# Moving nearly all 128x128 transposes from TensorE to the DMA engines, with two residual buffers and an earlier load of Wo

## The chip, the cores and the metric

One core of one Trainium2 chip runs the whole program in one launch. The metric is the device time in microseconds (us), and lower is better.

Engine names as the profile has them: PE is TensorE's matmul side, PEld its weight load, DVE is VectorE, ACT is ScalarE, POOL is GpSimd, SP is SyncE. SP issues the DMAs here, and "SPq" marks the time an issue holds SP's sequencer.

## The reference

The program is four layers on a sequence of 2048 tokens with 640 features, in the order A, B, A, B. Each is a residual layer on a layer norm.

```python
x = x + A(layernorm(x)); x = x + B(layernorm(x)); x = x + A(layernorm(x)); x = x + B(layernorm(x))

def A(x):                      # 32 heads of 20 features, 4 segments of 512 tokens
    for s in range(4):
        p = softmax(qs @ ks.T * scale + mask);  a_dot = p @ vs
        pq = phi(qs); a_mem = (pq @ M) / (pq @ z + 1e-6)
        o = g * a_mem + (1 - g) * a_dot         # g = sigmoid(beta), per head
        pk = phi(ks); M = M + pk.T @ vs; z = z + sum(pk)
    return o @ wo              # phi(t) = t + 1 if t > 0 else exp(t)

def B(x):                      # 32 heads of 128, 64 steps of 32 tokens, 8 memory tokens
    for s in range(64):
        h = concat(mem, xs); q, k, v = h @ Wq, h @ Wk, h @ Wv
        o = (softmax(q @ k.T * scale + mask) @ v) @ Wo
        mem = o[:8]; outs.append(o[8:])         # the next step needs this one's output
```

## The kernel before

Everything is bf16 except the accumulations. A layer A is 32 units, each one segment for four heads, and a unit is six slots. The kernel fixes the order of the instructions on PE, ACT, DVE and POOL. So an instruction that waits also holds up everything behind it on its engine, although nothing else in the program needs it (the timeline after the change shows such a case: ACT idle for 4.09 us before the exp of K, with the exp of the last scores behind it). SP is a fifth, in-order queue, which issues nearly all DMAs (in that unit the transpose of K is issued 3.28 us late, behind four others).

The projection of the next unit, and K's feature map with its transposes:

```python
def proj(u, k):                                   # k = 0: Q, k = 1: K
    PP = pg.tile([128, 512], F32, name="a_PP", tag="pg")
    for c in range(NCH):                          # NCH = 5
        nc.tensor.matmul(PP[:], lhsT=wts[u][k][:, c, :], rhs=xnTs[n % 2][:, c, :], ...)
    nc.vector.tensor_copy(U.qk[:, k, :], PP[:])   # "evacuation" of K when k = 1
    ...
def phi_k(u):                                     # not in the last segment
    KN = pg.tile([128, 4, 128], BF16, name="a_KN", tag="pg")
    for tt in range(4):
        nc.tensor.transpose(KN[:, tt, :], U.qk[:, 1, 128 * tt:128 * tt + 128], C.identb[:])
    EK = ...; nc.scalar.activation(out=EK[:], in_=KNv, func=ACT.Exp)
    t1 = ...; nc.vector.tensor_scalar(out=t1[:], in0=KNv, ...)          # max(k + 1, 1)
    nc.vector.tensor_tensor(out=phik[u % 2][...], in0=EK[:], in1=t1[:], op=ALU.min)
```

The schedule of a unit, with `extras` standing for norms, V projections and output projections that are spread over the slots:

```python
for slot in range(6):
    score(u, slot)                                # a_S on PE, exp into a_PT on ACT
    if slot == 0: proj(u + 1, 0)
    if slot == 1: pvmm(u - 1, 1); norm(u - 1)
    if slot == 2: proj(u + 1, 1); phi_q(u + 1)
    if slot == 4: pvmm(u, 0); phi_k(u + 1)
    if slot == 5: nummm(u); memory(u)             # a_UP on PE, then a_um on DVE
    extras(u, slot)
```

The PSUM pool `pg` is shared by `a_PP`, `a_KN`, `a_UP` and the transposes. Norms (`a_tps`), attention outputs (`a_otps`) and B's norms (`b_lntps`) are transposed on PE in the same way, then copied out of PSUM by ACT. B loads its residual into the one tile `XO` in mid-step, and holds the first 11 of 32 heads of Wo early (`NW1 = 11`).

Of the kernel before, what the change touches and what calls it, by code (L numbers as in the profile page):

```python
# [26 lines left out]
NW1 = 11  # L27
# [171 lines left out]
def layer_A(nc, nc_raw, tc, C, W, A_wv, A_wo, x_src, x_dst, xb_dst, src_is_bf16, general, outer, mem0, prep=None, prefetch=()):  # L199
# [5 lines left out]
    with ExitStack() as ctx:  # L205
# [19 lines left out]
        Onat = so.tile([128, 4, D], BF16, name="a_Onat")  # L225
# [41 lines left out]
        def ln_tr(nc, xn, n, tt):  # L267
            tps = pg.tile([128, NCH, 128], BF16, name="a_tps", tag="pg")
            for c in range(NCH):
                nc.tensor.transpose(tps[:, c, :], xn[:, 128 * c:128 * c + 128], C.identb[:])  # L270
            nc.scalar.copy(xnTs[n % 2][:, :, 128 * tt:128 * tt + 128], tps[:])
# [24 lines left out]
        eps = so.tile([128, 2, 4, 4], F32, name="a_eps")  # L296
# [3 lines left out]
        for tt in range(5):  # L300
            if tt < 4:
                stats[tt] = ln_stats(nc, xts[tt])
            if tt > 0:
                ln_tr(nc, ln_apply(nc.vector, xts[tt - 1], *stats[tt - 1]), 0, tt - 1)
# [9 lines left out]
        gg = W.gates(nc, so)  # L314
        build_masks(nc, C)

        def run(gctx):
# [14 lines left out]
            wl = wk1 if general else wk  # L332
# [15 lines left out]
            def phi_q(u):  # L348
                if u // NG == 0:
                    return  # L350
                U = us[u]
                t1 = wl.tile([128, 512], BF16, name="a_t1q", tag="t1")
                nc.vector.tensor_scalar(out=t1[:], in0=U.qk[:, 0, :], scalar1=1.0, scalar2=1.0, op0=ALU.add, op1=ALU.max)
                nc.vector.tensor_tensor(out=U.phiq[:], in0=U.phiq[:], in1=t1[:], op=ALU.min)

            def phi_k(u):
                if u // NG == NS - 1:
                    return
                U = us[u]
                KN = pg.tile([128, 4, 128], BF16, name="a_KN", tag="pg")  # L360
                for tt in range(4):
                    nc.tensor.transpose(KN[:, tt, :], U.qk[:, 1, 128 * tt:128 * tt + 128], C.identb[:])
                KNv = KN[:].rearrange("p t (j s) -> p t j s", s=32)[:, :, :, 0:20]
                EK = wl.tile([128, 4, 4, 20], BF16, name="a_EK")
                nc.scalar.activation(out=EK[:], in_=KNv, func=ACT.Exp)
                t1 = wl.tile([128, 4, 4, 20], BF16, name="a_t1k", tag="t1")
                nc.vector.tensor_scalar(out=t1[:], in0=KNv, scalar1=1.0, scalar2=1.0, op0=ALU.add, op1=ALU.max)
                nc.vector.tensor_tensor(out=phik[u % 2][:, :, :, 0:20], in0=EK[:], in1=t1[:], op=ALU.min)

            def row_max(u):  # L370
# [19 lines left out]
                ms = wl.tile([12, 512], BF16, name="a_ms", tag="t1")  # L390
# [58 lines left out]
            def norm(u):  # L449
                n, G = divmod(u, NG)  # L450
                K = 2 if n else 1
                pv = us[u].pv
                r = so2.tile([128, 2, 4, 4], F32, name="a_r")
                nc.vector.tensor_tensor(out=r[:, 0:K], in0=pv[:, 0:K, :, :, 20], in1=eps[:, 0:K], op=ALU.add)
                i = so2.tile([128, 2, 4, 4], F32, name="a_i")
                nc.vector.reciprocal(out=i[:, 0:K], in_=r[:, 0:K])
                if not general:
                    watch(nc, C, r[:, 0].rearrange("p t j -> p (t j)"), i[:, 0].rearrange("p t j -> p (t j)"))
                q = so2.tile([128, 2, 4, 4], F32, name="a_q")
                nc.vector.tensor_tensor(out=q[:, 0:K], in0=i[:, 0:K], in1=gg[:, 0:K, 4 * G:4 * G + 4].unsqueeze(2).to_broadcast([128, K, 4, 4]), op=ALU.mult)  # L460
                Ov = Onat[:, :, 80 * G:80 * G + 80].rearrange("p t (j d) -> p t j d", d=20)
                if n == 0:
                    nc.vector.tensor_tensor(out=Ov, in0=pv[:, 0, :, :, 0:20], in1=q[:, 0].unsqueeze(3).to_broadcast([128, 4, 4, 20]), op=ALU.mult)
                else:
                    ts = so.tile([128, 2, 16, 20], F32, name="a_ts")
                    nc.vector.tensor_tensor(out=ts[:].rearrange("p k t d -> p (k t) d"), in0=pv[:].rearrange("p k t j s -> p (k t j) s")[:, :, 0:20],
                                            in1=q[:].rearrange("p k t j -> p (k t j)").unsqueeze(2).to_broadcast([128, 32, 20]), op=ALU.mult)
                    tv = ts[:].rearrange("p k (t j) d -> p k t j d", j=4)
                    nc.gpsimd.tensor_tensor(out=Ov, in0=tv[:, 0], in1=tv[:, 1], op=ALU.add)
                us.pop(u)  # L470

            def memory(u):
# [9 lines left out]
                else:  # L482
                    um = wk1.tile([128, 4, 21], F32, name="a_um", tag="a_EK" if general else "a_um")
# [4 lines left out]
            def chunk(c):  # L488
                tps = pg.tile([128, 4, 128], BF16, name="a_otps", tag="pg")
                for tt in range(4):  # L490
                    nc.tensor.transpose(tps[:, tt, :], Onat[:, tt, 128 * c:128 * c + 128], C.identb[:])
                nc.scalar.copy(oT[:, c, :], tps[:].rearrange("p t q -> p (t q)"))
# [28 lines left out]
            def bridge_ops(G, slot):  # L521
# [15 lines left out]
                if (G, slot) == (5, 4):  # L537
                    xn, m0 = ln["b"]
                    tps = pg.tile([128, NCH, 128], BF16, name="a_btps", tag="pg")
                    for c in range(NCH):  # L540
                        nc.tensor.transpose(tps[:, c, :], xn[:, 128 * c:128 * c + 128], C.identb[:])
                    nc.scalar.copy(br.xnT[:], tps[:])
# [16 lines left out]
            def extras(u, slot):  # L559

                n, G = divmod(u, NG)
                if n >= 1 or u >= NU:
                    if (G, slot) == (0, 0):
                        chunk(3)
                        if u < NU:
                            res_load(n - 1, 0); res_load(n - 1, 1)
                    elif (G, slot) == (1, 0):
                        chunk(4)
# [10 lines left out]
                seq = {(4, 0): 0, (5, 0): 1, (6, 0): 2}  # L579
                if (G, slot) in seq:  # L580
                    chunk(seq[G, slot])
# [19 lines left out]
            proj(0, 0); proj(0, 1); phi_q(0); phi_k(0)  # L601
            if general:
                row_max(0)
            for u in range(NU + 1):
# [7 lines left out]
                for slot in range(6):  # L612
# [7 lines left out]
                    if slot == 2 and more:  # L620
                        proj(u + 1, 1)
                        phi_q(u + 1)
# [10 lines left out]
            br.tail = [lambda: chunk(4)] + [lambda i=i: outp(NS - 1, i) for i in range(8)]  # L633
# [27 lines left out]
def layer_B(nc, nc_raw, tc, C, W, br, outer, wo_src, x_src, xb_src, x_dst, general, nsteps=64, out_bf16=False):  # L661
# [4 lines left out]
    with ExitStack() as ctx:  # L666
# [43 lines left out]
        def ln_tr(g):  # L710
            xn = ln_n.pop(g)
            tps = pot.tile([128, NCH, 128], BF16, name="b_lntps", tag="ot")
            for c in range(NCH):
                nc.tensor.transpose(tps[:, c, :], xn[:, 128 * c:128 * c + 128], C.identb[:])
            xg = wk2.tile([128, NCH, 128], BF16, name="b_xnTg")
            nc.scalar.copy(xg[:], tps[:])
# [157 lines left out]
        XO = st.tile([64, 320], F32, name="b_XO")  # L874
        nc.vector.memset(XO[:], 0.0)
# [38 lines left out]
        for a, b in ((NW1, 22), (22, 32)):  # L914
# [18 lines left out]
        for s in range(nsteps):  # L933
            last = (s == nsteps - 1)
            T, i4 = divmod(s, 4)
            if i4 == 0 and T >= 1:
                load_deferred(T - 1)
# [182 lines left out]
            for jj2 in range(2):  # L1120
                nc.sync.dma_start(XO[32 * jj2:32 * jj2 + 24, :], x_src[32 * s:32 * s + 24, 320 * jj2:320 * jj2 + 320])
# [51 lines left out]
            def store(s=s, ops=ops):  # L1173
# [123 lines left out]
```

## Time and profile before

| | before |
|---|---|
| median (lowest to highest) of its 4 runs | 2296.64 us (2293.05 to 2297.84) |
| profiled run (2302.5 us, another run than these four): span, mean granted clock | 2300.8 us, 0.981 |
| first A, first B, second A, second B | 263.2, 830.9, 266.1, 846.1 us |
| the two joins from A to B | 22.0, 21.1 us |

The stage lengths are worked out from the timeline. An A runs from its first to its last score matmul (`a_S`), a join from there to B's first matmul (`b_Qa`), and what is missing from the span is the start of the program and the passage from B to A (28.5 and 22.9 us).

The page of the kernel before: busy time by engine, PE's granted clock in 40 slices of the span, in tenths (9 is full or nearly so), and the chain of waits that ended last, by engine.

```profile
PE 2195.3 (95%) x54988; PEld 1234.9 (54%) x54988; DVE 1623.6 (71%) x3996; ACT 961.6 (42%) x2207; POOL 1028.5 (45%) x2475
...
PEclk9999989999999999999999999999999999999999
...
PE 81%; DVE 8%; ACT 5%; issue 3%; DMA 2%; SPq 1%; POOL 0%; DVEq 0%; ACTq 0%; POOLq 0%
```

At 95% PE looks like the only limit. By windows it is not. The next fence has the first A, the first join with most of the first B, and the second A of the kernel before. The columns are the window, its length, and busy us (with instructions) of PE, PEld, DVE, ACT and POOL, then PE's granted clock, the DMA share and GB/s.

```profile
28.50:291.70 263.20, 241.28 (x2747) 128.40 (x2747) 193.37 (x490) 199.51 (x276) 118.61 (x301) 0.97 0.53 150
293.00:1140.00 847.00, 836.75 (x24538) 475.70 (x24539) 601.32 (x1459) 275.05 (x818) 389.06 (x926) 0.99 0.10 28
1167.60:1433.60 266.00, 243.67 (x2746) 129.07 (x2746) 195.28 (x484) 197.38 (x270) 116.32 (x280) 0.96 0.34 107
```

In B, PE is nearly full (836.75 of 847 us here). In A it is idle for 22 us of each layer, and no other engine is full. There the unit is a cycle of waits through PE, DVE and ACT. The timeline of one unit of the second A shows it (start, duration, engine, line, operation, written and read tiles, count, and in brackets the idle time before it and what ended it).

```profile
1251.19 0.68 DVE L85 CAST a_qk<-a_PP 128x512 bf16<-128x512 f32 x1
...
1252.25 0.38 PE L85 MATMUL a_KN<-c_identb,a_qk 128*128 128x128 bf16 x4
...
1252.67 0.44 ACT L85 ACTIVATE a_EK<-a_KN 128x320 bf16<-128x320 bf16 x1
...
1253.00 0.81 ACT L85 ACTIVATE a_PT<-a_S 128x768 bf16<-128x768 f32 x1
...
1253.85 0.42 DVE L85 TENSOR_TENSOR a_PT<-a_PT,a_tri 128x512 bf16<-128x512 bf16 x1
...
1254.19 0.24 DVE L85 TENSOR_TENSOR a_um<-a_UP,a_bd 128x84 f32<-128x84 f32 x1
...
1254.61 1.25 PE L85 MATMUL a_PP<-a_xnT,a_wt 128*128 128x512 bf16 x5
```

K is evacuated at 1251.87 (1251.19 plus 0.68). PE transposes it, and ACT's exp of K starts at 1252.67, 0.80 us after the evacuation. Behind it on ACT is the exp of the last scores (1253.00 to 1253.81), and behind that on DVE the mask (1253.85) and `a_um` (1254.19), which frees a PSUM buffer for the next projection `a_PP`. Five projection matmuls take 1.25 us here.

### The profile page before, as it was taken

How to read it: one execution, taken by the hardware profiler on the slowest of the kernel's cores; microseconds unless marked ns; L12 is line 12 of the kernel's file. 1: busy time of each engine (PE TensorE's matmuls, PEld its weight loads, DVE VectorE, ACT ScalarE, POOL GpSimd, SP SyncE). 2: the span in 40 equal slices, each digit the busy share in tenths (PEclk: the TensorE clock that was granted, in tenths of full speed). 3: DMA queues.
4: the chain of work that ended last, by engine and by line, in shares of the span. 5: the costliest groups of instructions: out<-in, count | busy, mean ns of one | idle time of the engine just before them, and what ended most of it. 6: DMA issues, size and time to landing. Idle time of an engine off the chain costs nothing.

```text
span 2300.8 us, 123029 instructions
## 1 busy us (share of the span) xinstructions
PE 2195.3 (95%) x54988; PEld 1234.9 (54%) x54988; DVE 1623.6 (71%) x3996; ACT 961.6 (42%) x2207; POOL 1028.5 (45%) x2475
## 2 busy tenths in 40 slices
PE   6998989999999999999889989899999999999997
PEld 3444545555555555555445445455555555555554
DVE  5777757777777777776667777577777777777775
ACT  5777823333333333333267667233323333333332
POOL 3344534444444444444323445344444444444442
PEclk9999989999999999999999999999999999999999
DMA  6455540000000000000123333400000000000000
GB/s 168 138 147 166 164 143 21 20 21 19 20 19 20 20 22 20 22 15 18 49 89 119 105 108 119 147 19 15 18 15 17 16 19 16 17 18 16 14 13 15
DMA packets 90652, 123.40 MB, mean 54 GB/s; under 512 B 16496, under 2 KB 80000, under 8 KB 88192
## 3 DMA queue, kind: packets, MB, share of 16 engines
q1 hardware_dynamic: 87648, 111.84, 16.9%
q8 instruction: 431, 7.06, 1.3%
q10 hardware_dynamic: 2464, 3.61, 0.6%
q14 instruction: 109, 0.89, 0.1%
HBM read 89.17 MB, written 26.21 MB: 50 GB/s over the span
## 4 chain that ended last, share of the span: by engine, by line
PE 81%; DVE 8%; ACT 5%; issue 3%; DMA 2%; SPq 1%; POOL 0%; DVEq 0%; ACTq 0%; POOLq 0%
PE b_V L85 13%; PE b_OPS L85 12%; PE b_tail L85 10%; PE b_Qa L85 6%; PE b_Kb L85 6%; PE b_Ka L85 6%; PE b_Qb L85 6%; PE b_SP L85 5%; PE a_PP L85 4%; ACT a_PT L85 4%; PE b_OTL L85 3%; PE b_OPSd L85 3%; PE a_S L85 2%; PE a_pv L85 2%; DVE a_qk L85 1%
## 5 line engine op out<-in xcount | busy, mean ns | idle before, releaser
L85 PEld LDWEIGHTS <-b_hT 128*32 128x32 bf16 x15120 | 372.3, 96 | 311.3 <-DVE b_hT L85 69.2
L85 ACT ACTIVATE b_PT<-b_SP 128x224 bf16<-128x224 f32 x256 | 92.3, 361 | 765.5 <-PE b_SP L85 744.7
L85 PE MATMUL b_V<-b_wv,b_hT 128*32 128x512 bf16 x5040 | 356.3, 381 | 0.0
L85 ACT ACTIVATE a_PT<-a_S 128x768 bf16<-128x768 f32 (+1 forms) x384 | 326.4, 893 | 62.8 <-PE a_S L85 56.1
L85 PE MATMUL b_OPS<-b_wo,b_OTsb 128*32 128x320 bf16 x8192 | 329.3, 302 | 6.5 <-DVE b_OTsb L85 5.1
L85 PEld LDWEIGHTS <-b_OTsb 128*32 128x32 bf16 x8192 | 200.4, 97 | 94.9 <-DVE b_OTsb L85 47.5
L85 POOL CAST b_QT<-b_TQ 128x384 bf16<-128x384 f32 x254 | 140.3, 552 | 231.5 <-DVE b_TQ L85 231.5
L85 ACT CAST b_OTsb<-b_OTL 128x320 bf16<-128x320 f32 x384 | 150.9, 427 | 198.9 <-PE b_OTL L85 183.1
L85 POOL TENSOR_TENSOR b_PT<-b_PT,b_R 128x64 bf16<-128x64 bf16 x256 | 107.3, 419 | 221.8 <-ACT b_R L85 197.4
L85 POOL CAST b_KT<-b_TQ 128x384 bf16<-128x384 f32 x254 | 142.6, 561 | 136.8 <-DVE b_TQ L85 132.1
L85 PE MATMUL b_Qa<-b_wq,b_hT 128*32 128x512 bf16 x2520 | 183.2, 384 | 5.0 <-DVE b_hT L85 5.0
L85 POOL TENSOR_SCALAR_AFFINE_SELECT a_PT<-a_PT 128x256 bf16<-128x256 bf16 x256 | 108.2, 424 | 174.2 <-ACT a_PT L85 162.1
L85 PE MATMUL b_Kb<-b_wk,b_hT 128*32 128x512 bf16 x2520 | 182.9, 380 | 0.1
L85 PE MATMUL b_Ka<-b_wk,b_hT 128*32 128x512 bf16 x2520 | 182.2, 382 | 0.0
L85 DVE STREAM_TRANSPOSE b_TM<-b_OPS 128x128 f32<-128x128 f32 x252 | 88.2, 350 | 123.6 <-PE b_OPS L85 119.7
L85 PE MATMUL b_Qb<-b_wq,b_hT 128*32 128x512 bf16 x2520 | 158.3, 379 | 0.0
L85 PE MATMUL a_PP<-a_xnT,a_wt 128*128 128x512 bf16 x560 | 146.5, 394 | 5.1 <-DVE a_um L85 1.3
L85 PE MATMUL a_S<-a_qk 32*128 32x512 bf16 (+3 forms) x1024 | 137.2, 308 | 8.1 <-ACT a_PT L85 6.9
L85 DVE CAST b_Vsb<-b_V 128x512 bf16<-128x512 f32 x128 | 88.6, 692 | 76.8 <-PE b_SP L85 48.0
L85 DVE CAST b_OTsb<-b_OTL 128x320 bf16<-128x320 f32 x128 | 62.9, 492 | 98.2 <-PE b_OTL L85 98.2
L85 DVE TENSOR_TENSOR b_PT<-b_PT,b_R 128x160 bf16<-128x160 bf16 x256 | 104.0, 406 | 37.7 <-PE b_V L85 18.6
L85 POOL TENSOR_TENSOR b_Rtot<-b_Rtot,b_R 128x160 bf16<-128x160 bf16 x256 | 126.6, 494 | 0.0
(165 smaller groups left out, 4276.0 us busy)
## 6 DMA issues: line engine op xcount, KB each, us to landing
a_wt<-a_wpad SPq DMA_DIRECT2D x112, 160.0 KB
b_XO<-xres SPq DMA_DIRECT2D x256, 30.0 KB
a_wvo<-in_A_wo_dram SPq DMA_DIRECT2D x8, 800.0 KB
b_wq<-in_B_Wq_dram SPq DMA_DIRECT2D x20, 256.0 KB
b_wk<-in_B_Wk_dram SPq DMA_DIRECT2D x20, 256.0 KB
xres<-a_xo SPq DMA_DIRECT2D x16, 320.0 KB
xres_bf<-a_xb SPq DMA_DIRECT2D x32, 160.0 KB
b_wv<-in_B_Wv_dram SPq DMA_DIRECT2D x20, 256.0 KB
```

The source lines that it names most:

```text
L85: r = f(*a, **k)
```

## The change

The intent is to free PE of its transposes and ACT of the copies behind them. Every norm in A (but those of the prologue), every K, all attention outputs, and the norms in B go through a transposing DMA on SP, 136 in all, from SBUF to SBUF. B's residual has two buffers, loaded at the start of a step, and 16 heads of Wo are loaded early instead of 11. Tiles move between pools to make room. The core of the diff, with cuts marked:

```diff
-NW1 = 11
+NW1 = 16
 ...
-        def ln_tr(nc, xn, n, tt):
+        def ln_tr(nc, xn, n, tt, dma=True):
+            dst = xnTs[n % 2][:, :, 128 * tt:128 * tt + 128]
+            if dma:
+                nc_raw.sync.dma_start(dst, xn[:], transpose=True)
+                return
 ...
+            def k_nat(u):
+                if u // NG == NS - 1:
+                    return
+                us[u].KN = (wk1 if general else wk).tile([128, 4, 128], BF16, name="a_KN")
+                nc_raw.sync.dma_start(us[u].KN[:], us[u].qk[:, 1, :], transpose=True)
 
             def phi_k(u):
 ...
-                KN = pg.tile([128, 4, 128], BF16, name="a_KN", tag="pg")
-                for tt in range(4):
-                    nc.tensor.transpose(KN[:, tt, :], U.qk[:, 1, 128 * tt:128 * tt + 128], C.identb[:])
-                KNv = KN[:].rearrange(...)
-                EK = wl.tile([128, 4, 4, 20], BF16, name="a_EK")
-                nc.scalar.activation(out=EK[:], in_=KNv, func=ACT.Exp)
+                KNv = us[u].KN[:].rearrange(...)
+                pk = phik[u % 2][:, :, :, 0:20]
+                nc.scalar.activation(out=pk, in_=KNv, func=ACT.Exp)
 ...
-            def chunk(c):                       # attention outputs, by PE and ACT
-                ...
+            def o_turn(tt):
+                nc_raw.sync.dma_start(oT[:, :, 128 * tt:128 * tt + 128], Onat[:, tt, :], transpose=True)
 ...
                     if slot == 2 and more:
                         proj(u + 1, 1)
+                        k_nat(u + 1)
                         phi_q(u + 1)
 ...
         def ln_tr(g):                           # layer B
 ...
-                nc.tensor.transpose(tps[:, c, :], xn[:, 128 * c:128 * c + 128], C.identb[:])
 ...
-            nc.scalar.copy(xg[:], tps[:])
+            nc.sync.dma_start(xg[:], xn[:], transpose=True)
 ...
+            XO = XOs[s % 2]
+            for jj2 in range(2):
+                nc.sync.dma_start(XO[32 * jj2:32 * jj2 + 24, :], x_src[...])     # was in mid-step
```

K's DMA is issued in slot 2 of the unit before, and its readers (`phi_k`) stay in slot 4.

More of the change, by code (lines that the diff above doesn't have):

```diff
@@ L224, in layer_A @@
         xnTs = [st.tile([128, NCH, 512], BF16, name=f"a_xnT{i}") for i in range(2)]
-        Onat = so.tile([128, 4, D], BF16, name="a_Onat")
+        Onat = st.tile([128, 4, D], BF16, name="a_Onat")
         oT = so.tile([128, NCH, 512], BF16, name="a_oT")
@@ L270, in ln_tr @@
                 nc.tensor.transpose(tps[:, c, :], xn[:, 128 * c:128 * c + 128], C.identb[:])
-            nc.scalar.copy(xnTs[n % 2][:, :, 128 * tt:128 * tt + 128], tps[:])
+            nc.scalar.copy(dst, tps[:])
         def vproj(nc, n, tt, half, eng="dve"):
@@ L295, in layer_A @@
             nc.vector.memset(bd[32 * j:32 * j + 32, j, :], 1.0)
-        eps = so.tile([128, 2, 4, 4], F32, name="a_eps")
+        eps = st.tile([128, 2, 4, 4], F32, name="a_eps")
         nc.vector.memset(eps[:, 0], 0.0)
@@ L303, in layer_A @@
             if tt > 0:
-                ln_tr(nc, ln_apply(nc.vector, xts[tt - 1], *stats[tt - 1]), 0, tt - 1)
+                ln_tr(nc, ln_apply(nc.vector, xts[tt - 1], *stats[tt - 1]), 0, tt - 1, dma=False)
         nc.gpsimd.affine_select(out=tri[:], in_=tri[:], pattern=[[1, 128]], compare_op=ALU.is_ge,
@@ L313, in layer_A @@
                 vproj(nc, 0, tt, half, ("dve", "act")[half])
-        gg = W.gates(nc, so)
+        gg = W.gates(nc, st)
         build_masks(nc, C)
@@ L331, in run @@
             us, xin = {}, {}
-            wl = wk1 if general else wk
             def proj(u, k):
@@ L351, in phi_q @@
                 U = us[u]
-                t1 = wl.tile([128, 512], BF16, name="a_t1q", tag="t1")
+                t1 = wk1.tile([128, 512], BF16, name="a_t1q", tag="t1")
                 nc.vector.tensor_scalar(out=t1[:], in0=U.qk[:, 0, :], scalar1=1.0, scalar2=1.0, op0=ALU.add, op1=ALU.max)
                 nc.vector.tensor_tensor(out=U.phiq[:], in0=U.phiq[:], in1=t1[:], op=ALU.min)
+            def k_nat(u):
[3 more added lines that the diff above has]
+                nc_raw.sync.dma_start(us[u].KN[:], us[u].qk[:, 1, :], transpose=True)
             def phi_k(u):
@@ L358, in phi_k @@
                     return
-                U = us[u]
-                KN = pg.tile([128, 4, 128], BF16, name="a_KN", tag="pg")
-                for tt in range(4):
-                    nc.tensor.transpose(KN[:, tt, :], U.qk[:, 1, 128 * tt:128 * tt + 128], C.identb[:])
-                KNv = KN[:].rearrange("p t (j s) -> p t j s", s=32)[:, :, :, 0:20]
-                EK = wl.tile([128, 4, 4, 20], BF16, name="a_EK")
-                nc.scalar.activation(out=EK[:], in_=KNv, func=ACT.Exp)
-                t1 = wl.tile([128, 4, 4, 20], BF16, name="a_t1k", tag="t1")
+                KNv = us[u].KN[:].rearrange("p t (j s) -> p t j s", s=32)[:, :, :, 0:20]
+                pk = phik[u % 2][:, :, :, 0:20]
+                nc.scalar.activation(out=pk, in_=KNv, func=ACT.Exp)
+                t1 = wk1.tile([128, 4, 4, 20], BF16, name="a_t1k", tag="t1")
                 nc.vector.tensor_scalar(out=t1[:], in0=KNv, scalar1=1.0, scalar2=1.0, op0=ALU.add, op1=ALU.max)
-                nc.vector.tensor_tensor(out=phik[u % 2][:, :, :, 0:20], in0=EK[:], in1=t1[:], op=ALU.min)
+                nc.vector.tensor_tensor(out=pk, in0=pk, in1=t1[:], op=ALU.min)
             def row_max(u):
@@ L389, in row_max @@
                     nc.tensor.transpose(mt[:, qc, :], parts[:, qc].rearrange("p j i -> p (j i)"), C.identb[:])
-                ms = wl.tile([12, 512], BF16, name="a_ms", tag="t1")
+                ms = wk1.tile([12, 512], BF16, name="a_ms", tag="t1")
                 nc.vector.tensor_copy(ms[:], mt[:].rearrange("p q t -> p (q t)"))
@@ L452, in norm @@
                 pv = us[u].pv
-                r = so2.tile([128, 2, 4, 4], F32, name="a_r")
+                r = wk.tile([128, 2, 4, 4], F32, name="a_r")
                 nc.vector.tensor_tensor(out=r[:, 0:K], in0=pv[:, 0:K, :, :, 20], in1=eps[:, 0:K], op=ALU.add)
-                i = so2.tile([128, 2, 4, 4], F32, name="a_i")
+                i = wk.tile([128, 2, 4, 4], F32, name="a_i")
                 nc.vector.reciprocal(out=i[:, 0:K], in_=r[:, 0:K])
@@ L458, in norm @@
                     watch(nc, C, r[:, 0].rearrange("p t j -> p (t j)"), i[:, 0].rearrange("p t j -> p (t j)"))
-                q = so2.tile([128, 2, 4, 4], F32, name="a_q")
+                q = wk.tile([128, 2, 4, 4], F32, name="a_q")
                 nc.vector.tensor_tensor(out=q[:, 0:K], in0=i[:, 0:K], in1=gg[:, 0:K, 4 * G:4 * G + 4].unsqueeze(2).to_broadcast([128, K, 4, 4]), op=ALU.mult)
@@ L464, in norm @@
                 else:
-                    ts = so.tile([128, 2, 16, 20], F32, name="a_ts")
+                    ts = wk1.tile([128, 2, 16, 20], F32, name="a_ts")
                     nc.vector.tensor_tensor(out=ts[:].rearrange("p k t d -> p (k t) d"), in0=pv[:].rearrange("p k t j s -> p (k t j) s")[:, :, 0:20],
@@ L482, in memory @@
                 else:
-                    um = wk1.tile([128, 4, 21], F32, name="a_um", tag="a_EK" if general else "a_um")
+                    um = wk1.tile([128, 4, 21], F32, name="a_um", tag="t1" if general else "a_um")
                     nc.vector.tensor_tensor(out=um[:], in0=UP[:, :, 0:21], in1=bd[:], op=ALU.mult)
@@ L486, in memory @@
                 nc.gpsimd.tensor_copy(MZb[:, G], MZ32[:, G])
-            def chunk(c):
-                tps = pg.tile([128, 4, 128], BF16, name="a_otps", tag="pg")
-                for tt in range(4):
-                    nc.tensor.transpose(tps[:, tt, :], Onat[:, tt, 128 * c:128 * c + 128], C.identb[:])
-                nc.scalar.copy(oT[:, c, :], tps[:].rearrange("p t q -> p (t q)"))
+            def o_turn(tt):
+                nc_raw.sync.dma_start(oT[:, :, 128 * tt:128 * tt + 128], Onat[:, tt, :], transpose=True)
             def res_load(n, tt):
@@ L538, in bridge_ops @@
                     xn, m0 = ln["b"]
-                    tps = pg.tile([128, NCH, 128], BF16, name="a_btps", tag="pg")
-                    for c in range(NCH):
-                        nc.tensor.transpose(tps[:, c, :], xn[:, 128 * c:128 * c + 128], C.identb[:])
-                    nc.scalar.copy(br.xnT[:], tps[:])
+                    nc_raw.sync.dma_start(br.xnT[:], xn[:], transpose=True)
+                if (G, slot) == (6, 0):
+                    m0 = ln["b"][1]
                     v = br.xnT[:].rearrange("p c (i t) -> p c i t", t=32)
@@ L563, in extras @@
                     if (G, slot) == (0, 0):
-                        chunk(3)
                         if u < NU:
                             res_load(n - 1, 0); res_load(n - 1, 1)
-                    elif (G, slot) == (1, 0):
-                        chunk(4)
+                    elif (G, slot) in ((0, 4), (0, 5)):
+                        o_turn(2 * slot - 8); o_turn(2 * slot - 7)
                     else:
@@ L578, in extras @@
                     bridge_ops(G, slot)
-                seq = {(4, 0): 0, (5, 0): 1, (6, 0): 2}
-                if (G, slot) in seq:
-                    chunk(seq[G, slot])
                 if n + 1 < NS:
@@ L600, in run @@
                 wload(0); wload(1)
-            proj(0, 0); proj(0, 1); phi_q(0); phi_k(0)
+            proj(0, 0); proj(0, 1); k_nat(0); phi_q(0); phi_k(0)
             if general:
@@ L632, in run @@
                     row_max(u + 1)
-            br.tail = [lambda: chunk(4)] + [lambda i=i: outp(NS - 1, i) for i in range(8)]
+            br.tail = [lambda i=i: outp(NS - 1, i) for i in range(8)]
         with ExitStack() as gctx:
@@ L711, in ln_tr @@
             xn = ln_n.pop(g)
-            tps = pot.tile([128, NCH, 128], BF16, name="b_lntps", tag="ot")
-            for c in range(NCH):
-                nc.tensor.transpose(tps[:, c, :], xn[:, 128 * c:128 * c + 128], C.identb[:])
             xg = wk2.tile([128, NCH, 128], BF16, name="b_xnTg")
-            nc.scalar.copy(xg[:], tps[:])
+            nc.sync.dma_start(xg[:], xn[:], transpose=True)
             xnT_g[g] = xg
@@ L873, in layer_B @@
             nc.vector.memset(Rtot[:], 0.0)
-        XO = st.tile([64, 320], F32, name="b_XO")
-        nc.vector.memset(XO[:], 0.0)
+        XOs = [st.tile([64, 320], F32, name=f"b_XO{i}") for i in range(2)]
+        for t in XOs:
+            nc.vector.memset(t[:], 0.0)
         if general:
@@ L913, in layer_B @@
         wo.append(wop2.tile([128, 32 - NW1, D], BF16, name="b_wo2"))
-        for a, b in ((NW1, 22), (22, 32)):
+        for a, b in ((NW1, 24), (24, 32)):
             nc_raw.sync.dma_start(wo[1][:, a - NW1:b - NW1, :], wo_src[:, a:b, :])
@@ L935, in layer_B @@
             T, i4 = divmod(s, 4)
+            XO = XOs[s % 2]
+            for jj2 in range(2):
+                nc.sync.dma_start(XO[32 * jj2:32 * jj2 + 24, :], x_src[32 * s:32 * s + 24, 320 * jj2:320 * jj2 + 320])
             if i4 == 0 and T >= 1:
@@ L1119, in layer_B @@
                 late.pop(0)()
-            for jj2 in range(2):
-                nc.sync.dma_start(XO[32 * jj2:32 * jj2 + 24, :], x_src[32 * s:32 * s + 24, 320 * jj2:320 * jj2 + 320])
             scores(1)
@@ L1172, in layer_B, with store @@
                 ln_dma((s + 7) // 4)
-            def store(s=s, ops=ops):
+            def store(s=s, ops=ops, XO=XO):
                 xo = add_out(ops, XO, "b_xnb")
```

## The prediction

> **What bounds the kernel now.** The page: PE 95% busy over 2301 us at a granted clock of 0.98; the chain of waits that ended last is 81% PE. Busy time by windows splits it. The two B layers (about 293–1140 and 1435–2300 us) have PE at 99.7–100%. The two A layers (about 295 us each) have PE near 92%, ACT 70%, DVE 75%: there no engine is full, and a cycle of waits binds.
>
> That cycle, from the timeline of an A unit (185–194 us; units start 8.4 us apart): the projection of K ends, DVE evacuates it late (behind the norm and a mask, done at 187.93), PE transposes it at once (188.30), ACT's `a_EK` runs at 188.72, then ACT's exp of the last scores (to 189.86), DVE's mask and `a_um` (to 190.48), which frees the PSUM buffer that the next unit's projection takes at 190.66. From evacuated K to `a_EK` is 0.8 us today, with no slack. In the first segment (units 6.4 us apart) ACT is nearly full instead, and the slack there is about 1.2 us.
>
> **What the change removes (groups by shape, timeline).**
> - B: 150 `b_lntps` transposes. Five hold PE 0.39 us (365.65 to 366.04): 30 x 0.39 = 11–12 us on a full PE, so real gain.
> - A: 192 `a_KN`, 160 `a_otps`, 120 of 160 `a_tps`. Four hold PE about 0.3 us: some 36 us of PE at most, but only part lies on the cycle. The `a_xnT` copy (0.69 us) does sit between `a_EK` and the exp in 24 units: about 15 us. In all 20 us gain in A.
> - The two XO buffers: DVE waits for the `b_XO` load 2.4 us in all. Wo early: PE waits 1.3 us for it. Both about nothing.
>
> **What it adds.** 128 or 160 KB transposing DMAs on the one in-order SP queue, about 0.35 us or more to issue (plain DMAs take 0.32–0.45 us there). The K one is on the cycle: evacuated K, issue, transfer, completion, then `a_EK`, in engine order, holds up the exp behind it. [...] The trace's first plain 160 KB load is issued at 0.8 us and used at 4.9. I estimate 2.5–3 us from evacuated K to `a_EK`, instead of 0.8. That lengthens about 12 units per layer by the whole 1.7–2.2 us, the other four of segments 1 and 2 by less, and the eight of the first segment by 1–1.5 us: 30–40 us per layer, 60–80 in all. The last segment has no K transpose.
>
> **Sum.** +60–80, minus 20 (A), minus 12 (B), some us either way at the layer joins: +30–45, against a fair chance that the DMA is quicker. Predicted 2325 us, 2258 to 2410. Faster by over 2%: 0.12; within 2%: 0.48; slower by over 2%: 0.40.
>
> **What would show it.** B steps 0.4 us shorter where a norm was transposed; A layers longer, segments 1 and 2 most, the last segment slightly shorter; the list of waits shows ACT (the K exp writing `a_phik`) and DVE `a_t1k` waiting for the DMA of `a_KN`, 1.5–2 us each, 48 times; PE in A below 90%.
>
> **What would make it wrong.** A DMA transpose under 1.5 us end to end: then about 2255. Or one much slower (4 us or more, or stuck behind the weight prefetches of the first A layer): then the attention-output transposes too hold up `a_YP`, and 2400 is passed.

It was one of the grounds for the 2.5–3 us from evacuated K to `a_EK`. The traced load (issued at 0.8 us, used at 4.9, so 4.1 us) and the plain issues (0.32–0.45 us) don't give 2.5–3 us by themselves: it stands as the author's estimate, and so does what is built on it (1.7–2.2 us per unit, 60–80 us in all). 60 to 80, minus 20, minus 12, is +28 to +48 us, put down as +30–45. "ACT is nearly full" in the first segment fits its start (10.24 us busy of the 11.5 from 28.5 us on) better than the whole (48.89 of the 61.5 us up to 90).

## More of the kernel before

The kernel before takes about 2296 us. It was measured again on the same chip beside every group of experiments, since it isn't quite the same everywhere (medians of 2296 to 2303 us).

Over the 48 units with a K transpose, evacuation to exp takes 0.49 to 2.03 us, 0.84 in the mean.

## The result and the profile after

| | before | after |
|---|---|---|
| median (lowest to highest), 4 runs each | 2296.64 (2293.05 to 2297.84) | 2424.51 (2422.38 to 2427.36) |
| ratio, 95% interval | | 1.056 [1.0542, 1.0579]: slower |
| profiled run: span, mean granted clock | 2300.8, 0.981 | 2425.6, 0.932 |
| first A, first B, second A, second B | 263.2, 830.9, 266.1, 846.1 | 310.3, 826.5, 341.6, 838.0 |
| the two joins from A to B | 22.0, 21.1 | 26.8, 31.3 |

A ratio is the mean time of one kernel's runs over the mean of the other's runs of the same rounds, so it is not quite the ratio of the medians quoted.

The loss is in A: +47.1 and +75.5 us. The joins add 4.8 and 10.2, and B gives back 4.4 and 8.1. That makes 125 us with the rest unchanged, which is the difference of the spans. By segments the second A went from 60.8, 75.4, 75.0 and 54.8 us to 88.8, 101.7, 98.4 and 52.7. The last segment, which has no K transpose, is 2 us shorter.

The page of the kernel after, the same lines as before:

```profile
PE 2215.7 (91%) x54294; PEld 1224.7 (50%) x54356; DVE 1622.5 (67%) x3998; ACT 909.7 (38%) x2111; POOL 1025.8 (42%) x2475
...
PEclk9788889999999999999867787889999999999999
...
PE 78%; DMA 8%; DVE 5%; ACT 4%; issue 3%; SPq 1%; POOL 1%; ACTq 0%; DVEq 0%; POOLq 0%
```

PE has fewer instructions and yet more busy time, and in most slices of A its granted clock is at 0.6 to 0.8. The DMA is now 8% of the chain of waits. The two A layers of the kernel after by windows:

```profile
28.10:338.40 310.30, 249.43 (x2487) 120.30 (x2518) 189.56 (x490) 183.25 (x245) 118.57 (x302) 0.83 0.59 151
1214.60:1556.20 341.60, 265.45 (x2486) 123.16 (x2517) 192.31 (x484) 181.12 (x239) 115.65 (x280) 0.77 0.40 105
```

Window length minus PE's busy time is PE's idle time: 22 and 22 us before, 61 and 76 after. Two things have grown, then: idle time, and the length of PE's own instructions. The clock records of the trace hold only two values, full clock and half (1.0 and 0.5), so a mean of 0.77 is about 46% of the window at half clock.

The list of waits of the kernel after (engine and written tile, what it waited for, us in total, times, longest):

```profile
DVE a_t1k L85 <- DMA a_KN<-a_qk: 140.0, 48, 5.6
...
ACT a_phik L85 <- DMA a_KN<-a_qk: 124.4, 46, 5.5
...
PE a_PP L85 <- DVE a_um L85: 54.0, 20, 4.6
...
PE a_S L85 <- ACT a_PT L85: 43.6, 42, 4.4
...
DVE b_TQ L85 <- DMA a_oT<-a_Onat: 13.9, 2, 7.0
```

The three DMA lines are not in the list of the kernel before, when these tiles had no DMA. The two PE lines and the exp's wait for K stood there at:

```profile
ACT a_EK L85 <- PE a_KN L85: 12.6, 13, 3.3
...
PE a_S L85 <- ACT a_PT L85: 6.9, 25, 0.3
...
PE a_PP L85 <- DVE a_um L85: 1.3, 8, 0.2
```

In the list of the kernel after, the first two lines are the direct cost. The next two are how it reaches PE: the projection waits for the PSUM buffer that `a_um` frees, and the scores wait for the buffer that the exp frees. The last line is the joins: B's first evacuation on DVE (`b_TQ`) starts only when the transposed outputs of the last segment have landed, 7 us of waiting each time.

One unit of the second A in the timeline of the kernel after:

```profile
1308.56 2.32 PE L85 MATMUL a_PP<-a_xnT,a_wt 128*128 128x512 bf16 x5
...
1309.59 5.17 SPq L494 DMA_TRANSPOSE a_oT<-a_Onat  x4
...
1310.91 0.69 DVE L85 CAST a_qk<-a_PP 128x512 bf16<-128x512 f32 x1 [0.57 <-PE a_PP L85]
...
1314.88 1.20 SPq L363 DMA_TRANSPOSE a_KN<-a_qk  x1
...
1317.33 0.47 ACT L85 ACTIVATE a_phik<-a_KN 128x320 bf16<-128x320 bf16 x1 [4.09 <-DMA a_KN<-a_qk]
1317.40 0.24 DVE L85 TENSOR_SCALAR a_t1k<-a_KN 128x320 bf16<-128x320 bf16 x1 [5.14 <-DMA a_KN<-a_qk]
...
1318.55 0.50 PE L85 MATMUL a_S<-a_qk 32*128 32x384 bf16 x2 [1.97 <-ACT a_PT L85]
```

K is evacuated at 1311.60. SP is busy with four output transposes until 1314.76, so K's DMA is issued 3.28 us late. It holds SP for 1.20 us, its readers start about 1.25 us after that, and the exp of K starts 5.73 us after the evacuation. ACT sat idle for 4.09 us, DVE for 5.14, and PE for 1.97 behind the exp of scores that follows on ACT. And the five projection matmuls took 2.32 us, not 1.25, at half clock (0.50 granted from 1308 to 1311 us).

Over all units of the kernel after, evacuation to exp takes at least 2.47 us, in the mean 3.26 in the first A and 4.29 in the second, and at most 6.62. The issue comes 0.49 and 0.91 us after the evacuation in the mean.

### The profile page after: what moved, and what is told of

It reads as the page before. It is cut to its first block, busy times and chain, and to the rows that moved or that the text cites. A ratio compares the mean times of both kernels' runs of the same rounds, so it can differ in the third digit from the quotient of the medians.

```text
span 2425.6 us, 121898 instructions
## 1 busy us (share of the span) xinstructions
PE 2215.7 (91%) x54294; PEld 1224.7 (50%) x54356; DVE 1622.5 (67%) x3998; ACT 909.7 (38%) x2111; POOL 1025.8 (42%) x2475
## 3 DMA queue, kind: packets, MB, share of 16 engines
q1 hardware_dynamic: 172896, 132.57, 21.4%
## 4 chain that ended last, share of the span: by engine, by line
PE 78%; DMA 8%; DVE 5%; ACT 4%; issue 3%; SPq 1%; POOL 1%; ACTq 0%; DVEq 0%; POOLq 0%
PE b_V L85 12%; PE b_OPS L85 12%; PE b_tail L85 8%; PE b_Qa L85 6%; PE b_Kb L85 6%; PE b_Ka L85 6%; PE b_Qb L85 6%; PE a_PP L85 5%; DMA a_KN<-a_qk 5%; PE b_SP L85 4%; ACT a_PT L85 4%; PE b_OTL L85 3%; PE b_OPSd L85 3%; PE a_S L85 2%; PE a_pv L85 2%
## 5 line engine op out<-in xcount | busy, mean ns | idle before, releaser
L85 PEld LDWEIGHTS <-b_hT 128*32 128x32 bf16 x15120 | 377.8, 96 | 309.8 <-DVE b_hT L85 69.5
L85 PE MATMUL a_PP<-a_xnT,a_wt 128*128 128x512 bf16 x505 | 176.8, 477 | 83.4 <-DVE a_um L85 54.0
L85 PE MATMUL a_S<-a_qk 32*128 32x512 bf16 (+3 forms) x1024 | 154.6, 345 | 47.4 <-ACT a_PT L85 43.6
L85 PEld LDWEIGHTS <-a_wt 128*128 128x128 bf16 x560 | 55.6, 111 | 161.3 <-issue 134.9
```

The source lines that it names most:

```text
L85: r = f(*a, **k)
```

## The experiments

Theories before the first experiments. **K latency**: the loss is K's DMA on the cycle of the unit. **Rival 1, contention**: all the transposing DMAs together (SP's queue, the joins) cost the time, and K alone would cost much less. **Rival 2, the clock**: it falls by itself, for PE has fewer instructions. A third rival: **pool moves**, the single buffers (and the exp written in place) that the change needed for room. Later a second part was asked about: how much of the loss is the clock, which was lower where PE idled more (0.83 and 0.77 in the A layers after, with 61 and 76 us of idle time, against 0.97 and 0.96 with 22 and 22 before). Every kernel below gave the reference's result. The edits are shown condensed: lines are joined, and guards and the program's start are left out.

### K back on PE

The kernel after, with K's transposes as before.

```diff
-                proj(u + 1, 1); k_nat(u + 1)
+                proj(u + 1, 1)
 def phi_k(u):
+    KN = pg.tile([128, 4, 128], BF16, name="a_KN", tag="pg")
+    for tt in range(4):
+        nc.tensor.transpose(KN[:, tt, :], us[u].qk[:, 1, 128 * tt:128 * tt + 128], C.identb[:])
```

> The changed kernel with only the K transposes back on PE; outputs, norms, Wo and XO stay as changed. Theory (the K DMA's latency sits on the cycle of an A unit): segments 0 to 2 of each A layer fall from 76/94/88 and 89/102/98 us back to about 61/72/70, no wait of a_t1k or of the K exp on a DMA, granted clock in A back to 0.95 or so, and the total comes to 2285-2305 us. Rival 1 (the four output transposes, 5.2 us of SP each time, and the SP queue as a whole are to blame): the total stays above 2350. Rival 2 (the clock falls by itself, for fewer PE instructions): the clock in A stays near 0.80 and the total above 2350.

Measured: 2264.55 us against 2303.34 for the kernel before, ratio 0.9846 [0.9816, 0.9876]. The two A layers of this kernel by windows:

```profile
29.10:274.50 245.40, 226.54 (x2581) 117.90 (x2610) 192.22 (x490) 182.80 (x245) 118.61 (x301) 0.98 0.71 178
1149.80:1390.20 240.40, 223.73 (x2581) 116.96 (x2610) 192.51 (x484) 180.52 (x239) 116.22 (x281) 1.00 0.49 135
```

Undoing this one part takes 65 and 101 us off the two A layers, 166 in all, and leaves A 18 and 26 us shorter than before. All pool moves, all other transposing DMAs and the longer joins (27.8 and 31.8 us) are still there. So the pool moves fall, and rival 1 falls as the main cause. Rival 2 falls as well: the clock in A is back at 0.98 and 1.00, with fewer PE instructions than before the change. The time was below the expected range, since the gain of the other parts in A had been underrated. In these traces the 166 us are 65 us of longer PE busy time (514.9 against 450.3 us in the two layers) and 101 us of more idle time.

### The kernel before with K alone by DMA

```diff
-    nc.tensor.transpose(KN[:, tt, :], ...)          # four of them
+    nc_raw.sync.dma_start(us[u].KN[:], us[u].qk[:, 1, :], transpose=True)     # issued in slot 2
```

> The kernel before with the K transposes alone by DMA (t1 in one buffer, for space, as in the change). Theory: nearly all of the loss is here, with less queueing on SP than in the whole change: K arrives 2.5 to 3 us after its evacuation, segments 0 to 2 lengthen by 10 to 25 us each, total 2370-2420 us. Rival 1 (output transposes and queueing to blame): under 2330 us. No saving in B and none at the layer joins.

Measured: 2432.17 us, ratio 1.0553 [1.0515, 1.0591]. In total this is as much as the whole change lost, and above the expected range. The A layers take 320.0 and 336.1 us, 127 us more than before. Another 11 us are in the first B and come from a wait of its own (see the last experiment). With SP nearly free of other transposes, evacuation to exp is 2.79 and 3.33 us in the mean, less than in the kernel after. The units are as long all the same. The copies of transposed norms are still on ACT here, behind the exp of K, and PE waits 50.1 us in all for them before its V projections, a wait that the list of the kernel before doesn't have:

```profile
PE a_VP L85 <- ACT a_xnT L85: 50.1, 18, 4.5
```

So K's DMA alone is enough, even without a queue of other transposes: its issue came 0.06 and 0.15 us after the evacuation in the mean. It also shows that the price of K's DMA depends on the order of the count: 127 us in A when it is added to the kernel before (the rest of the change then gains only 4 more), 166 when it is taken out of the kernel after.

### K's feature map later, two ways

If the cost is only that the DMA hasn't landed when ACT and DVE come to it, its readers can be moved. `phik_late` moves `phi_k` from slot 4 of the unit before to slot 3 of its own unit, five slots later. `phik_split` puts the exp in slot 2 and DVE's part in slot 4 of the own unit.

```diff
-    if slot == 4: pvmm(u, 0); phi_k(u + 1)
+    if slot == 3: phi_k(u)                            # phik_late
+    if slot == 2: phi_k_exp(u)                        # phik_split
+    if slot == 4: pvmm(u, 0); phi_k_min(u)            # phik_split
```

> The changed kernel with the exp and min on K moved from slot 4 of the unit before to slot 3 of its own unit; every DMA stays. phik is needed in slot 5 of its own unit only. Theory (latency on the cycle, not traffic): a K that lands 2.5 to 5.7 us after its evacuation is in time, the waits of 140 and 124 us on a_KN fall below 20 us each, and the total is 2255-2290 us, faster than both kernels. Rival (DMA or SP throughput, or the output transposes): the waits move to other places and the total stays above 2350.

> The changed kernel with the exp on K in slot 2 of its own unit and the DVE part (a_t1k and min) in slot 4 of it, instead of both in slot 3 as in phik_late (2308 us). Theory: in phik_late no wait on the DMA was left; its remaining loss against K on PE (2265) came from where the pair was put: DVE waited 1 us for the exp and evacuations behind it came late. Split, 2255-2285 us. Rival (the K DMAs themselves cost, by SP time or traffic): stays at 2300 or above.

Measured: 2308.13 us, ratio 1.0018 [0.9990, 1.0045], and 2304.79 us, ratio 1.0040 [1.0007, 1.0073]. Both expectations were missed: about 40 us stay lost against K on PE. The list of waits of `phik_late` shows why:

```profile
PE a_UP L85 <- DVE a_phik L85: 28.8, 38, 1.2
...
ACT a_phik L85 <- DMA a_KN<-a_qk: 0.2, 1, 0.2
```

The DMA waits are gone (124.4 us to 0.2). But now the feature map is finished just before the memory update in slot 5 of the same unit needs it, so PE waits for DVE: 28.8 us here, and 31.7 us in the same line of `phik_split`. PE's clock in A is at 0.90 and 0.92 in `phik_late`. Taking the wait for the DMA away gave back most of the loss, and made a shorter wait elsewhere.

### Both one unit later

So the memory update has to move too: `phi_k` of a unit to slot 4 of its own unit, and `memory` of the unit before to slot 5. The result stays the same: what `memory` writes is read again only in the next segment, eight units on. Three kernels: the kernel after with this, the same with the last segment's outputs on PE (for the joins), and a control with K's transposes on PE too.

```diff
-    if slot == 4: pvmm(u, 0); phi_k(u + 1)
-    if slot == 5: nummm(u); memory(u)
+    if slot == 4: pvmm(u, 0); phi_k(u)
+    if slot == 5: nummm(u); memory(u - 1)
```

> The changed kernel with both the feature map of K (exp, t1k, min) and the memory update that reads it put off by one whole unit, each in the slot it had (4 and 5). phik_late and phik_split removed the DMA wait but made PE's a_UP wait for a_phik (0.8 us, 40 times in phik_split). Theory: latency was the whole cost of K by DMA, so with neither wait left the A layers come to 240-250 us each and the total to 2255-2275 us (ratio 0.982-0.990). Rival (the K DMAs cost SP time or traffic that hurts elsewhere): 2290 us or more, with waits on SP or other DMAs to show for it.

> unit_later with the last segment's output transposes on PE, as in k_back_o_join (2255 us). Theory: 10 us less than unit_later from the joins, 2240-2260 us. Rival: as for unit_later.

> Control: the same schedule as unit_later_o_join, but K transposed by PE. Theory: if K by DMA is free once its latency is hidden, the DMA kernel beats this one by PE's and PSUM's part, 192 transposes of 0.08 us or some 5-15 us; this one comes to 2245-2260 us. Rival: this one is the faster.

Measured: 2282.88 us, ratio 0.9931 [0.9908, 0.9955]; 2275.18 us, ratio 0.9899 [0.9875, 0.9923]; control 2260.47 us, ratio 0.9822 [0.9796, 0.9848]. The first two missed their ranges. The control came 0.5 us above its own, and its theory failed: it beats both DMA kernels, where the theory had the DMA kernel ahead by 5 to 15 us. The two A layers by windows, first K by DMA (with the joins mended), then the control:

```profile
28.20:296.50 268.30, 232.77 (x2529) 116.42 (x2530) 190.42 (x490) 183.37 (x247) 118.84 (x301) 0.92 0.70 174
1168.30:1408.50 240.20, 222.10 (x2528) 114.31 (x2529) 190.76 (x484) 180.96 (x242) 116.32 (x280) 0.98 0.61 149
```

```profile
28.10:280.70 252.60, 231.75 (x2624) 119.47 (x2625) 191.79 (x490) 183.78 (x247) 118.24 (x301) 0.96 0.69 173
1156.20:1397.80 241.60, 226.07 (x2625) 117.75 (x2626) 192.69 (x484) 181.64 (x242) 116.44 (x281) 0.99 0.49 135
```

In the second A the DMA now costs nothing that one trace of each can show: 240 against 242 us. So it was the place of the latency on the cycle, and not the transfer as such, that cost 101 us there. The first A still loses 16 us against its control. That layer also prefetches B's weights, and in it PE waits 6.2 us for the DMA of `a_xnT` and 1.3 us for that of `a_oT`, two waits that the control's first A doesn't have. So contention on SP or the DMA engines fits. No run tested it, and it stays open.

### Useless matmuls to keep the clock

To weigh the clock by itself: the kernel after, with 20 matmuls of 160 columns at the start of each unit of the first three segments, written to PSUM columns that nothing reads.

```diff
+if slot == 0 and u >= 1 and u // NG < NS - 1:
+    for _ in range(20):
+        nc.tensor.matmul(us[u - 1].pv[:, 0, :, :, 22:32], lhsT=C.identb[:], rhs=us[u].qk[:, 0, 0:160], ...)
```

> The changed kernel plus 20 matmuls of 160 columns without use, in each A unit of segments 0 to 2, placed where PE waits for the next projection's buffer (they write unused columns of a_pv). Theory: part of the loss is second hand, PE's granted clock falls to half because PE idles; keeping PE busy lifts the clock in A from 0.80 to 0.9 or more and the total falls by 15 to 40 us, to 2385-2410 (ratio 1.038-1.050). Rival (the clock follows but costs nothing, the DMA wait alone sets the time): total unchanged at 2424 or longer by up to 60 us.

Measured: 2399.59 us, ratio 1.0451 [1.0427, 1.0475], within the expectation. The A layers by windows:

```profile
28.80:325.50 296.70, 263.67 (x2977) 148.76 (x2978) 189.27 (x490) 182.15 (x245) 119.67 (x302) 0.94 0.63 158
1200.40:1523.10 322.70, 274.97 (x2977) 151.76 (x2978) 191.20 (x484) 180.31 (x239) 116.57 (x281) 0.90 0.42 111
```

Extra work made the kernel about 25 us faster (2424.51, 2399.59, each 2296 before). The clock rose from 0.83 and 0.77 to 0.94 and 0.90, while the waits of ACT and DVE for K's DMA hardly changed (133 and 130 us in total, 124 and 140 without the useless work). So the half clock is a real part of the loss, and those 25 us are best read as its least size. How much larger it is, this run can't say: the kernel is still 4.5% slower than before, but the useless matmuls themselves added 78 us of busy time to PE, and part of that time is on the cycle too.

### Attention outputs back on PE

> The changed kernel with only the attention outputs back on PE (as before the change); K and the norms stay on DMA. Theory: bursts of four output transposes (5.2 us of SP, four times per layer) delay only one or two K transposes per segment and cost about 5 to 10 us at each join of A to B, so 2395-2415 us against 2424 (ratio 1.043-1.052), joins back to 22 us. Rival (the SP queue's load by output transposes is the main cost): below 2340 us.

```diff
-    o_turn(tt)                    # four transposing DMAs per segment
+    chunk(c)                      # PE transposes and an ACT copy, in the slots they had before
```

Measured: 2412.67 us, ratio 1.0491 [1.0446, 1.0536], within the expectation. The joins are back at 22.0 and 22.7 us, as before, while A is no shorter (312.2 and 346.5). So the outputs' DMAs cost the joins 13 us in all. Taking their 5 us of SP time per segment away shortened evacuation to exp only to 2.88 and 4.04 us in the mean. That the PE and ACT work which came back ate this up fits, but isn't shown. The queue of output transposes is not what makes A slow as a whole.

### K on PE, and the last segment's outputs on PE

> k_back_on_pe (2265 us) with the last segment's output transposes on PE too, so that DMA transposes are left only where nothing waits for them. Joins measured 27.8 and 31.8 us with them by DMA, 22.0 and 21.1 before. Theory: joins return to 22 us, the last segment pays 1.5-2 us for them, total 2250-2258 us (ratio 0.978-0.982). Rival (joins are long for another reason, such as Wo's loads): joins and total unchanged.

Measured: 2254.75 us, ratio 0.9814 [0.9790, 0.9838], as expected, and 1.9% faster than the kernel before. It is the lowest median of all, but its interval overlaps those of K on PE alone and of the control. The A layers take 251.3 and 244.0 us and the joins 21.4 and 22.4. In the profiled runs the joins gained 15.9 us on K on PE alone, and the A layers lost 9.5. Only 2.5 of these are in the last segments, where the edit acts; the other 7 show how far two traces can differ where nothing was changed. This version takes the part of the change that doesn't wait (norms, outputs of the first three segments, B) and leaves PE the transposes that are needed at once.

### B's norms alone by DMA, with one and with two residual buffers

The kernel before, with only B's 30 norm transposes by DMA. The second kernel adds the two `XO` buffers and their early load.

```diff
-    nc.tensor.transpose(tps[:, c, :], xn[:, 128 * c:128 * c + 128], C.identb[:])   # five
-    nc.scalar.copy(xg[:], tps[:])
+    nc.sync.dma_start(xg[:], xn[:], transpose=True)
```

> The kernel before with only B's 30 norm transposes by DMA. Theory: 0.39 us of a full PE each, so 11-12 us less, all in the B layers (831 to 827 and 846 to 838 in the two traces): 2283-2287 us. Rival (B's gain came from the two XO buffers or Wo early): 2293-2297.

> b_norm_dma_alone (2303 us, ratio 1.000) plus the two XO buffers. Its trace had the norm steps 0.4 us shorter, as predicted, but every eighth step up to 1.3 us longer, DVE waiting for the b_XO load. Theory: the second buffer takes that wait away, the 11-12 us then show: ratio 0.993-0.996, 2281-2288 us. Rival (XO does nothing): ratio 1.000 again.

Measured over 5 rounds: 2303.00 us, ratio 0.9999 [0.9978, 1.0021], a miss; and 2294.19 us, ratio 0.9980 [0.9962, 0.9998], short of its range. In the first, the steps with a transpose are 0.4 us shorter as predicted (from one step's first `b_Qa` to the next, a median of 12.66 and 12.63 us in the two B layers instead of 13.07). But in its first B other steps are longer: every eighth one has a median of 14.13 us where the kernel before has 12.62. (The text says up to 1.3 us longer; step against step it is 1.0 to 2.6.) The trace of the K-alone kernel, whose B is the unchanged one, has the same steps in its first B, and shows what happens in one:

```profile
773.04 1.01 DVE L85 TENSOR_TENSOR b_XO<-b_OPS,b_XO 64x320 f32<-64x320 f32 x2 [2.22 <-DMA b_XO<-xres]
...
774.86 0.62 PE L85 MATMUL b_Kb<-b_wk,b_hT 128*32 128x512 bf16 x8 [1.34 <-DVE b_TQ L85]
```

The two issues of the residual's load held SP for 2.02 us, from 769.54, and it lands late: DVE waits 2.22 us for it, and PE 1.34 us behind DVE. In all DVE waits 10.8 us for `b_XO` in the norms-alone kernel and 12.7 in the K-alone one, against 2.4 in the profile of before. With two buffers the wait is gone and those steps are normal. So the buffers, which I had valued at nothing, took away what ate B's gain in these traces; in the times, the intervals of the two kernels overlap. What brings this wait into some kernels with the same B and not into the one before is open. Both traces that have it were taken on the same chip (6), and the kernel before wasn't traced there, so the chip is a rival. Two-buffer kernels traced on that chip (K on PE, and `phik_late`) don't have it. Why the two-buffer kernel's B layers gained 4.6 us and not the 12.5 of the kernel after is partly seen: of the roughly 8 us between them, 6.6 lie in the first step of each B (20.9 and 21.9 us, against 18.3 and 18.0 with 16 heads of Wo held early), not in the norms.

## Why the prediction was wrong

**The kernel's limits and the direction: right.** A is a cycle of waits and not a full engine, the K transpose is on it, and its DMA sits there 48 times. The waits by DVE and ACT (48 and 46 of them, 2.9 and 2.7 us in the mean where 1.5 to 2 were written), PE below 90% in A (80 and 78%), the slightly shorter last segment, and B's steps 0.4 us shorter all came. "Segments 1 and 2 most" held only in the first A: its segments 0 to 2 went from 63.1, 73.9 and 71.5 us to 75.6, 93.9 and 87.9, a loss of 12.5, 20.0 and 16.4. In the second A they lost 28.0, 26.3 and 23.4, so the slack that I gave to segment 0 didn't save it.

**The step that failed** is the term "That lengthens about 12 units per layer by the whole 1.7–2.2 us ...: 30–40 us per layer, 60–80 in all". The runs put 166 us in its place, 65 and 101 (after, against the same kernel with K on PE), or 127 when K's DMA alone is added to the kernel before: by either count well above 80. The whole sum, term by term:

| term | predicted, us | measured, us | from |
|---|---|---|---|
| K by DMA | +60 to +80 | +166 | after minus K back on PE, A layers |
| gain in A by all the rest | −20 | −43 | K back on PE minus before, A layers |
| B | −12 | −12.5 | after minus before |
| joins | "some us either way" | +15 | after minus before |
| sum | +30 to +45 | +125 | profiled spans, 2425.6 − 2300.8 |

The term was too small for three reasons.

1. **The latency was taken as one number, and it was the best case.** I estimated "2.5–3 us from evacuated K". The least that was measured is 2.47 us, so as a floor it was good. But the mean was 3.26 and 4.29 us. An issue that I put at "0.35 us or more" held SP for 1.20 us. So K's DMA had to wait for SP, 0.49 and 0.91 us in the mean: mostly behind the transpose of a norm and a plain load, and once in each A behind a run of output transposes, for 3.0 and 3.3 us. The rest of the excess over the floor lies between the issue and the start of the exp, and the traces don't say why. If the extra 2.4 and 3.5 us over the mean of before (0.84) fell on all 24 units of a layer, that would be 58 and 83 us, an estimate that counts no slack.
2. **The clock wasn't in the sum at all.** With PE idle for some us per unit its granted clock was lower: 0.97 and 0.96 became 0.83 and 0.77, and the same five matmuls took 2.32 instead of 1.25 us. PE's busy time in A rose from 485 to 515 us with fewer instructions. The trace shows half clock after such idle time, as in the unit shown (0.50 from 1307 us on, after PE had been idle for 2.05 us up to 1305.88), and the useless matmuls put about 25 us or more on it. My text doesn't mention the clock.
3. **A wait on an ordered engine doesn't stay in its unit's slack.** In the K-alone kernel, with a mean latency of only 2.79 and 3.33 us, A lost 57 and 70 us, more than the extra latency of all 24 units adds up to (47 and 60 us). The engines behind the wait still had all their work to do; PE's 50.1 us of waits for norm copies are part of it. That this is the whole reason is argued, not shown.

How the 166 us divide by cause can't be settled by these runs, though in the traces they are 101 us of idle time and 65 us of longer busy time. The two go together in the runs: with the useless matmuls PE's idle time in the A layers was 33 and 48 us instead of 61 and 76 and its clock 0.94 and 0.90 instead of 0.83 and 0.77, and matmuls that take 2.32 instead of 1.25 us evacuate K later.

The gain in A was mis-sized too, in the other direction: it is about double what I wrote, though my 20 us even counted K's own transposes. No run takes it apart. It is only there when K isn't on the path: with K by DMA, the rest gains 4 us in A.

That B's term came out right is partly luck. I counted 30 norms of 0.39 us, but 3.4 of the 12.5 us came from the first step of each B, and the norms alone gained nothing that could be measured.

**"What would make it wrong"** named a DMA of 4 us or more "stuck behind the weight prefetches of the first A layer". In the kernel after it was the second A, without these prefetches, that lost more, and the K issue came mostly behind other transposes. I had the queue right and its contents mostly wrong. The 4 us did come there (4.29 in the mean) and 2400 was passed, but not as I wrote, by `a_YP` held up by the output transposes: PE's `a_YP` waited 2.0 us for them in all.

**Wo early and two buffers: "about nothing".** For Wo the first step of each B fell from 19.7 and 20.0 to 18.3 and 18.0 us, 3.4 us in all, which is small but a quarter of B's gain. The buffers do matter where the residual's load comes late, as shown.

## What to carry to other kernels

Ask of each operation that moves to another engine when its result is needed, and not only how busy the old engine was. Transposes with microseconds of slack (norms, outputs in mid-layer) together gained from the DMA (with K on PE, A was 43 us shorter than before), and those needed at once lost several times what PE saved (166 us, where PE had spent 48 times some 0.38 us, or 18 us, on them). Moving their readers a whole unit later won most of that back, but no more: the same schedule with K on PE was still faster (2260 against 2275 us).

Price an asynchronous step at its mean under the queue it will share, with the time it holds the issuing engine, and not at its floor (here 3.26 and 4.29 us, of which the issue held SP for 1.20, against a floor of 2.47). If PE will idle for microseconds per unit because of it, add the loss of PE's clock, as it was measured here (0.97 and 0.96 down to 0.83 and 0.77 in A, and about 25 us or more of the time).

## What was measured of the transposing DMA and of the clock

- **Time on the issuing engine.** The issue of a 128x512 transpose from SBUF to SBUF held SP for 1.19 to 1.31 us in 46 of the 48 cases of the kernel after (1.59 and 1.74 in the other two), about half of the 2.47 us from evacuated to used at the least, and four of 128x640 in a row held it for 5.17 us in the unit shown.
- **Against plain DMAs.** The issue takes longer than a plain one: 1.20 us here for 128 KB, against medians of 0.32 to 0.58 us, tile by tile, for plain DMAs of 160 KB on the same queue.
- **End to end.** The traces put evacuation to use of four blocks at 2.47 us by DMA at the least, and at 3.26 and 4.29 us in the mean with other transposes in the queue. On PE it is 0.49 us at the least, of which four transposes hold PE for 0.38.
- **The clock and short gaps.** In the kernel after, windows give PE a full clock from 1302 to 1307 us and a half one from there, and the timeline shows a single idle stretch of PE from 1300 to 1307, 2.05 us long (1303.83 to 1305.88). If no record is missing there, half clock came here after one gap of 2 us. It isn't a single case: of the 14 PE gaps of 1.9 to 3.0 us in that trace that began at full clock, 13 had a stretch of half clock begin within them or less than 2 us after them.
